# Chunks across four batches, states in place and one order table: a recurrence and a gated feed-forward layer in one kernel

## The chip, the cores and the metric

The kernel runs on one core of a Trainium2 chip. A core has TensorE (PE in the profile; PEld is its weight load), VectorE (DVE), ScalarE (ACT), GpSimd (POOL) and SyncE (SP), which here issues most of the DMAs. The engines run side by side, each through its own instructions in order, and wait for one another through semaphores. The metric is the device time of one execution in microseconds (us). The matrix products leave their results in PSUM, all else lies in SBUF.

## The reference

Inputs are `r`, `k`, `v`, `w` of shape (4 batches, 8 heads, 768 steps, 48) and `u`. A state of 48 x 48 per batch and head runs over the steps, and its output is the input of a gated feed-forward layer:

```python
state = np.zeros((B, H, D, D), dtype=np.float32)
for t in range(S):
    kt, vt, rt, wt = (k[:, :, t], v[:, :, t], r[:, :, t], w[:, :, t])
    cur = np.einsum('bhd,bhe->bhde', u[None] * kt, vt)
    y[:, :, t] = np.einsum('bhd,bhde->bhe', rt, state + cur)
    state = wt[:, :, :, None] * state + np.einsum('bhd,bhe->bhde', kt, vt)
x = y.transpose(0, 2, 1, 3).reshape(B * S, H * D)     # 3072 x 384
g = x @ w_gate                                        # 384 x 1536
return (g * (1.0 / (1.0 + np.exp(-g))) * (x @ w_val) @ w_out)
```

The weights of the layer come as 64-bit numbers.

## The kernel before

**Chunks.** The 768 steps of a batch are cut into 6 chunks of 128, so there are 24 chunks; chunk n here is chunk n % 6 of batch n // 6. The steps of a chunk, each a small function that takes n: loads `ws` (decays), `kr` (k and r, transposed), `nat` (k and r), `vt` (v); on VectorE `scan` (L287) and `scan2` (L304), running products of the decays from the end and from the start, between them `seed` (L296), which writes the reciprocal of the whole product into the first column of the tile `d1e`, from which `scan2` starts; `kq` and `re` scale k and r; ScalarE's `whole` keeps the whole product; `kb`, `kn` transpose k on TensorE and copy it out; `prod` (chunks 0 to 5) or `ru`, `ruk`, `a0` (the others) give the diagonal with `u`, `diag` (ScalarE) spreads it; `sc` (TensorE) makes the products of k and r, `pred` (VectorE) copies them over the diagonal under a mask; `sps` and `spb` decay the carried state and copy it for TensorE; `dl` and `st` add the chunk's part to it; `y` (TensorE) makes the chunk's output. `scan` reads the tile `d1q` and `scan2` the tile `d1e`; both are filled once.

**Products of the layer.** All products of the layer are made of two parts, a rounded value and its rest, in three matmuls. So `xh` (ScalarE) rounds `y` into the layer's input, and `xl` takes the rest, either on VectorE, or, for n < `TAKEN` = 10, by a matmul `xm` that subtracts the rounded part in PSUM and a copy on ScalarE. The 64-bit weights are turned into such pairs by the kernel, in 12 blocks f: `raw` (three DMAs), `top`, `low`, `upper` on ScalarE, `shift`, `sign`, `plus`, `lower` on VectorE. Two `raw` tiles take turns; one is free after `plus`.

**Groups.** The 24 chunks' outputs are put together in groups g of `GROUPS` = 4, 2, 4, 4, 4, 4, 2 tiles of 128 rows, as the moving side of the first products. For each group and each block f of 128 of the 1536 columns: `gv` (L534, 9 matmuls) twice, gate and value, 512 columns wide with four tiles and 256 with two; `silu` (ScalarE), `sg` (VectorE, times the value), `hh` and `hl` (the pair again), and `po` (L565), three matmuls of 384 columns for each tile, summed in PSUM over the 12 blocks. `ob` copies a finished tile out and `store` writes it. PSUM has two tiles for `gv`, four for `po` (lent to `sc` for the first four chunks), two for all of `kb`, `sc`, `dl` and `y`.

**Order.** `ORDER` (L47) names the steps in the order in which each engine and each DMA queue is to have them, for the start and groups 0 to 2. The steps that it names are kept in program order (`keep`, `pin`). `spin` are matmuls without use. From group 3 on, two Python loops (L624 to L654) issue the blocks, with the steps of the next group's chunks (`attention_steps`, `prepare`) between them; there only TensorE's order is pinned and the framework orders the rest. `check` takes the decays' bound for a flag; where the flag is set, a plain loop at the end computes all again. It overwrites `ws`, so for chunks 0 to 9 the loop loads `ws` a second time (`AGAIN`).

Of the kernel before, what the change touches and what calls it, by code (L numbers as in the profile page):

```python
# [52 lines left out]
scan:2 sign:1 whole:2 xh:1 vt:3 vz:2 kr:5 xm:1 spin:7 sps:2 xl:1 kq:2 spb:2 plus:1 kb:2 spin:5
seed:2 kn:2 raw:3 prod:3 upper:1 dl:2 spin:13 scan2:2 diag:2:1 st:2 ws:4 re:2 diag:2:0 lower:1
sc:2 spin:18 top:2 scan:3 low:2 pred:2:0 kq:3 vz:3 seed:3 whole:3 kb:3 pred:2:1 scan2:3 y:2 spin:4
kn:3 diag:3:0 shift:2 ws:5 re:3 vt:4 xh:2 sps:3 sc:3 diag:3:1 sign:2 xm:2 spin:8 spb:3 pred:3:0
xl:2 pred:3:1 top:3 dl:3 plus:2 y:3 spin:12 low:3 st:3 raw:4 scan:4 upper:2 vt:5 prod:4 xh:3
lower:2 vz:4 xm:3 spin:5 whole:4 xl:3 gv:0:0:0 kq:4 shift:3 seed:4 sign:3 gv:0:0:1 silu:0:0
scan2:4 top:4 plus:3 vz:5 ws:6 gv:0:1:0 low:4 re:4 raw:5 upper:3 sg:0:0 kb:4 scan:5 hh:0:0
gv:0:1:1 kn:4 lower:3 whole:5 diag:4:0 hl:0:0 diag:4:1 sc:4 seed:5 shift:4 po:0:0 sps:4 silu:0:1  # L60
sign:4 spb:4 top:5 sg:0:1 gv:0:2:0 plus:4 hh:0:1 low:5 hl:0:1 raw:6 pred:4:1 gv:0:2:1 upper:4
pred:4:0 silu:0:2 lower:4 po:0:1 sg:0:2 shift:5 hh:0:2 prod:5 dl:4 sign:5 gv:0:3:0 top:6 kq:5
low:6 st:4 gv:0:3:1 plus:5 hl:0:2 upper:5 raw:7 sps:5 kb:5 scan2:5 silu:0:3 po:0:2 nat:6 kn:5
diag:5:0 sg:0:3 ws:7 lower:5 hh:0:3 gv:0:4:0 hl:0:3 shift:6 re:5 po:0:3 silu:0:4 sign:6 top:7
scan:6 low:7 y:4 plus:6 whole:6 gv:0:4:1 diag:5:1 vt:6 seed:6 ru:6 raw:8 ruk:6 upper:6 a0:6 kr:6
gv:0:5:0 sg:0:4 nat:7 diag:6:0 lower:6 vz:6 hh:0:4 gv:0:5:1 shift:7 xh:4 spb:5 hl:0:4 sign:7
silu:0:5 po:0:4 top:8 sg:0:5 plus:7 hh:0:5 xm:4 gv:0:6:0 low:8 kq:6 raw:9 hl:0:5 upper:7 scan2:6
gv:0:6:1 silu:0:6 lower:7 ws:8 xl:4 re:6 sc:5 shift:8 po:0:5 sg:0:6 sign:8 hh:0:6 top:9 hl:0:6
gv:0:7:0 low:9 plus:8 scan:7 upper:8 raw:10 gv:0:7:1 pred:5:0 silu:0:7 whole:7 seed:7 lower:8
po:0:6 sg:0:7 shift:9 hh:0:7 gv:0:8:0 pred:5:1 sign:9 top:10 y:5 hl:0:7 low:10 plus:9 po:0:7  # L70
silu:0:8 kr:7 ru:7 upper:9 raw:11 ruk:7 a0:7 diag:6:1 lower:9 vt:7 kb:6 nat:8 gv:0:8:1 kn:6
shift:10 xh:5 diag:7:0 kq:7 xm:5 gv:0:9:0 sign:10 xl:5 sg:0:8 plus:10 hh:0:8 sc:6 top:11 gv:0:9:1
hl:0:8 pred:6:0 upper:10 pred:6:1 scan2:7 po:0:8 silu:0:9 low:11 lower:10 ws:9 vz:7 dl:6 ru:8 y:6
shift:11 gv:0:10:0 sg:0:9 diag:7:1 kr:8 vt:8 sign:11 hh:0:9 st:6 gv:0:10:1 plus:11 hl:0:9 upper:11
kb:7 re:7 po:0:9 silu:0:10 ruk:8 vz:8 lower:11 kn:7 a0:8 gv:0:11:0 sg:0:10 diag:8:0 nat:9 scan:8
hh:0:10 gv:0:11:1 sps:7 whole:8 kq:8 spb:7 seed:8 hl:0:10 scan2:8 silu:0:11 po:0:10 xh:6 ru:9
ws:10 re:8 ruk:9 xm:6 gv:1:0:0 sg:0:11 xl:6 a0:9 hh:0:11 gv:1:0:1 scan:9 nat:10 sc:7 hl:0:11
whole:9 seed:9 silu:1:0 po:0:11 pred:7:1 sg:1:0 pred:7:0 hh:1:0 ru:10 dl:7 ob:0:0 hl:1:0 gv:1:1:0
ob:0:1 ruk:10 out:0:0 out:0:1 st:7 y:7 sps:8 silu:1:1 po:1:0 diag:8:1 vt:9 kr:9 kb:8 gv:1:1:1
diag:9:0 a0:10 nat:11 gv:1:2:0 spb:8 sg:1:1 hh:1:1 gv:1:2:1 xh:7 hl:1:1 vz:9 silu:1:2 kn:8 po:1:1  # L80
sg:1:2 ob:0:2 kq:9 hh:1:2 out:0:2 xm:7 ob:0:3 gv:1:3:0 scan2:9 xl:7 out:0:3 sc:8 hl:1:2 ws:11 re:9
silu:1:3 po:1:2 ru:11 scan:10 gv:1:3:1 pred:8:1 whole:10 gv:1:4:0 seed:10 sg:1:3 ruk:11 hh:1:3
gv:1:4:1 pred:8:0 hl:1:3 dl:8 silu:1:4 po:1:3 st:8 sg:1:4 sps:9 hh:1:4 kb:9 y:8 hl:1:4 kn:9 po:1:4
diag:9:1 vt:10 kr:10 gv:1:5:0 diag:10:0 a0:11 gv:1:5:1 nat:12 silu:1:5 xh:8 gv:1:6:0 vz:10 sg:1:5
spb:9 xm:8 hh:1:5 gv:1:6:1 xl:8 hl:1:5 kq:10 silu:1:6 po:1:5 sg:1:6 scan2:10 hh:1:6 gv:1:7:0
hl:1:6 check:10 gv:1:7:1 ru:12 re:10 po:1:6 ruk:12 silu:1:7 ws:12 sg:1:7 scan:11 hh:1:7 gv:1:8:0
hl:1:7 gv:1:8:1 whole:11 seed:11 silu:1:8 gv:1:9:0 sg:1:8 hh:1:8 gv:1:9:1 hl:1:8 silu:1:9
gv:1:10:0 sg:1:9 gv:1:10:1 po:1:7 po:1:8 hh:1:9 hl:1:9 sc:9 silu:1:10 sg:1:10 hh:1:10 gv:1:11:0
pred:9:0 hl:1:10 gv:1:11:1 pred:9:1 silu:1:11 dl:9 sg:1:11 y:9 st:9 sps:10 po:1:9 spb:10 kr:11
vt:11 xh:9 po:1:10 hh:1:11 diag:11:0 hl:1:11 xm:9 po:1:11 xl:9 diag:10:1 kb:10 gv:2:0:0 kq:11  # L90
kn:10 a0:12 ob:1:0 scan2:11 nat:13 vz:11 ob:1:1 out:1:0 gv:2:0:1 silu:2:0 out:1:1 re:11 check:11
scan:12 gv:2:1:0 ws:13 sg:2:0 whole:12 seed:12 hh:2:0 ru:13 ruk:13 gv:2:1:1 hl:2:0 silu:2:1 po:2:0
sg:2:1 hh:2:1 hl:2:1 gv:2:2:0 po:2:1 silu:2:2 gv:2:2:1 gv:2:3:0 sg:2:2 hh:2:2 hl:2:2 gv:2:3:1
silu:2:3 po:2:2 sg:2:3 hh:2:3 hl:2:3 sc:10 po:2:3 pred:10:1 pred:10:0 dl:10 y:10 st:10 sps:11
gv:2:4:0 xh:10 kr:12 diag:12:0 vt:12 xl:10 spb:11 sc:11 silu:2:4 diag:11:1 gv:2:4:1 pred:11:0
kq:12 a0:13 vz:12 scan2:12 gv:2:5:0 nat:14 pred:11:1 check:12 re:12 kb:12 y:11 sg:2:4 kn:12 ws:14
scan:13 hh:2:4 gv:2:5:1 ru:14 whole:13 kr:13 diag:13:0 seed:13 vt:13 ruk:14 hl:2:4 xh:11 diag:12:1
xl:11 po:2:4 silu:2:5 a0:14 sg:2:5 nat:15 sc:12 kq:13 hh:2:5 vz:13 scan2:13 gv:2:6:0 hl:2:5
check:13 re:13 po:2:5 pred:12:0 silu:2:6 ws:15 pred:12:1 scan:14 dl:12 y:12 st:12 whole:14 seed:14
sps:13 kb:13 spb:13 kr:14 gv:2:6:1 vt:14 xh:12 kn:13 xl:12 diag:13:1 sc:13 sg:2:6 hh:2:6 gv:2:7:0  # L100
# [677 lines left out]
```

## Time and profile before

| | |
|---|---|
| three runs | 584.82, 585.49, 587.57 us; median 585.49 |
| the profiled execution: span | 585.2 us |
| mean granted TensorE clock | 0.993 |
| read from HBM, written | 45.04 MB, 4.72 MB |
| TensorE matmuls, spins among them | 5333, 160 |
| VectorE, ScalarE, GpSimd instructions | 511, 639, 11 |
| waits of VectorE's `sg` for `gv` | 138.3 us in 51 waits |
| waits of SP's `out` stores | 90.3 us for `ob` |

The page of the profile gives busy times over the whole span, a strip of 40 slices of 14.6 us each, and the groups of instructions. Matmuls are pipelined, so a matmul's own duration is longer than the time to the next one. The chain of waits, listed in order of time, merges runs of equal instructions: start, time, engine, line, count. A row of the timeline has start, duration, engine, line, operation, tiles and count. A row of a window has PE, PEld, DVE, ACT and POOL busy times with their counts, then the granted clock, DMA share and GB/s. A row of the waits has total us, number of waits and the longest.

### The profile page before, as it was taken

What the parts mean: (1) busy time and instruction counts of PE and PEld (TensorE: products, weight loads), DVE (VectorE), ACT (ScalarE), POOL (GpSimd) and SP (SyncE); (2) the same over time, 40 slices, a digit from 0 to 9 for tenths busy, and PEclk for the clock granted to TensorE, in tenths of its full rate; (3) what the DMA queues carried; (4) which work ended last, traced back from release to release, by engine and by line L of the source; (5) the groups of instructions that cost most, each with busy time, mean ns of one, the idle gap of its engine ahead of it and who ended that gap; (6) DMA issues with size and microseconds to landing.
All of it is one profiled execution on the core that took longest, in us unless ns stands there. A gap on an engine that the chain in (4) does not pass through costs nothing.

```text
span 585.2 us, 12525 instructions
## 1 busy us (share of the span) xinstructions
PE 570.4 (97%) x5333; PEld 494.4 (84%) x5333; DVE 325.1 (56%) x511; ACT 283.9 (49%) x639; POOL 1.8 (0%) x11
## 2 busy tenths in 40 slices
...
DVE  6999999995655349751456365446344332222221
...
GB/s 302 262 129 192 125 222 168 176 89 123 92 61 62 55 48 138 115 55 1 106 39 89 41 50 88 103 88 96 62 74 62 55 2 0 1 1 7 48 1 33
DMA packets 22334, 50.63 MB, mean 87 GB/s; under 512 B 2592, under 2 KB 8864, under 8 KB 22272
## 3 DMA queue, kind: packets, MB, share of 16 engines
...
q10 hardware_dynamic: 16, 0.00, 0.0%
HBM read 45.04 MB, written 4.72 MB: 85 GB/s over the span
## 4 chain that ended last, share of the span: by engine, by line
PE 83%; ACT 6%; DMA 5%; DVE 4%; issue 1%; SPq 0%; ACTq 0%; DVEq 0%
PE gv L541 46%; PE po L575 24%; PE y L441 5%; PE sc L385 4%; DMA raw<-in_wo_dram 2%; PE idle L608 2%; ACT at L346 1%; PE kb L361 1%; PE dl L409 1%; ACT raw L227 1%; DVE et L306 1%; DMA kr<-in_kr_dram 1%; DMA u_two<-in_u_rows_dram 1%; ACT raw L232 1%; ACT w_h L248 1%
## 5 line engine op out<-in xcount | busy, mean ns | idle before, releaser
L541 PE MATMUL gv<-xh,w_h 128*128 128x512 f32 (+1 forms) x504 | 183.7, 365 | 0.0
L541 PE MATMUL gv<-xl,w_h 128*128 128x512 f32 (+1 forms) x504 | 182.0, 361 | 0.0
L541 PE MATMUL gv<-xh,w_l 128*128 128x512 f32 (+1 forms) x504 | 181.6, 360 | 0.0
L553 DVE TENSOR_TENSOR sg<-sg,gv 128x512 f32<-128x512 f32 (+1 forms) x84 | 51.1, 608 | 141.4 <-PE gv L541 138.3
L541 PEld LDWEIGHTS gv<-xh,w_h 128*128 128x128 f32 x504 | 94.7, 188 | 15.1 <-issue 1.8
L541 PEld LDWEIGHTS gv<-xl,w_h 128*128 128x128 f32 x504 | 94.7, 188 | 15.0
L541 PEld LDWEIGHTS gv<-xh,w_l 128*128 128x128 f32 x504 | 94.8, 188 | 12.9
L575 PE MATMUL po<-w_h,hh 128*128 128x384 f32 x288 | 100.8, 350 | 0.5 <-ACT hh L558 0.5
L575 PE MATMUL po<-w_h,hl 128*128 128x384 f32 x288 | 97.2, 337 | 0.3 <-DVE hl L563 0.3
L558 ACT ACTIVATE hh<-sg 128x512 fp32r<-128x512 f32 (+1 forms) x84 | 47.8, 569 | 101.2 <-DVE sg L553 89.4
L575 PE MATMUL po<-w_l,hh 128*128 128x384 f32 x288 | 96.8, 336 | 0.0
L550 ACT ACTIVATE sg<-gv 128x512 f32<-128x512 f32 (+1 forms) x84 | 44.6, 531 | 90.8 <-PE gv L541 81.5
L563 DVE TENSOR_TENSOR hl<-sg,hh 128x512 fp32r<-128x512 f32 (+1 forms) x84 | 51.5, 613 | 51.1 <-ACT hh L558 50.7
L575 PEld LDWEIGHTS po<-w_h,hh 128*128 128x128 f32 x288 | 54.0, 188 | 7.5 <-issue 4.6
L575 PEld LDWEIGHTS po<-w_h,hl 128*128 128x128 f32 x288 | 54.1, 188 | 2.2 <-DVE hl L563 1.1
L575 PEld LDWEIGHTS po<-w_l,hh 128*128 128x128 f32 x288 | 54.0, 188 | 0.0
L346 ACT ACTIVATE at<-ident,a 128x128 f32<-128x128 f32 x144 | 45.6, 390 | 5.6 <-PE y L441 4.2
L390 DVE COPY_PREDICATED at<-mask,sc 128x512 f32<-128x512 uint32 x48 | 33.3, 730 | 8.7 <-PE sc L385 8.6
L317 ACT ACTIVATE ws<-ws 112x517 f32<-112x517 f32 x24 | 15.3, 638 | 35.3 <-DVE et L306 22.0
L289 DVE TENSOR_TENSOR_SCAN qt<-ws,d1q 112x516 f32<-112x516 f32 x24 | 29.4, 1226 | 1.8 <-DMA ws<-in_wt_dram 1.7
L306 DVE TENSOR_TENSOR_SCAN et<-ws,d1e 112x516 f32<-112x516 f32 x24 | 29.4, 1225 | 1.5 <-ACT pend L294 1.4
L385 PE MATMUL sc<-kr 48*64 48x128 f32 x768 | 28.6, 282 | 1.3 <-ACT kn L371 0.5
...
## 6 DMA issues: line engine op xcount, KB each, us to landing
...
raw<-in_gv_dram SPq DMA_DIRECT2D x24, 384.0 KB, 4.2
...
nat<-in_nat_dram SPq DMA_DIRECT2D x18, 384.0 KB, 3.1
raw<-in_wo_dram SPq DMA_DIRECT2D x12, 384.0 KB, 5.0
...
```

Source lines behind the costliest of these rows:

```text
L289: keep(nc.vector.tensor_tensor_scan(_flat(qts[n])[:, ::-1], wss[n][:, 1:][:, ::-1], _flat(d1q)[:, ::-1], 0.0, ALU.mult, ALU.add))
L306: keep(nc.vector.tensor_tensor_scan(_flat(ets[n]), wss[n][:, :L], _flat(d1e), 0.0, ALU.mult, ALU.add))
L346: keep(nc.scalar.activation(a[:, p, :], ident, AF.Copy, scale=d))
L385: pin(nc.tensor.matmul(scs[n][j][ms, p, :], krs[n][o, 0, p, ms], krs[n][o, 1, p, :], start=True, stop=True,))
L390: keep(nc.vector.copy_predicated(ats[n, j], mask4, scs[n][j]))
L441: pin(nc.tensor.matmul(ys[n][32 * q : 32 * q + 32, b // 4, :], lhs, rhs, start=start[q] == i, stop=stop[q] == i,))
L541: pin(nc.tensor.matmul(ps, a[:, f, j, q * P : (q + 1) * P], x[:, q, :], start=m == 0, stop=m == 3 * NK - 1,))
L550: keep(nc.scalar.activation(sgs[g, f], ps, AF.Silu))
L553: keep(nc.vector.tensor_tensor(sgs[g, f], sgs[g, f], gvs.pop((g, f, 1)), ALU.mult))
L558: keep(nc.scalar.activation(hhs[g, f], t, AF.Copy))
L563: keep(nc.vector.tensor_tensor(hls[g, f], t, hhs[g, f].bitcast(F32), ALU.subtract))
L575: pin(nc.tensor.matmul(pos[g][j], a[:, ts], x[:, f, 2, :], start=f == 0 and i == 0, stop=f == NF - 1 and i == 2,))
```

## The change

Chunk n now is chunk n // 4 of batch n % 4: the loads and the stores go through a list `place`, and the conditions on the chunk's place in its batch use n // 4. The four batches' states lie in four fixed tiles that `sps` and `st` change in place; `st` of the first four chunks is a copy on ScalarE. `ORDER` names all steps of the program to the last store, and the loops are gone. `TAKEN` is 6. In group 0 the first two blocks (f = 0, 1) are made in halves of 256 columns, `a` for tiles 0 and 1, `b` for tiles 2 and 3, and `po` can be named for one tile alone (`c0` to `c3`). One tile `d1` serves both scans: it holds ones in its last column, `seed` writes its first column, and a new step `zero` on GpSimd clears that column after `scan2`. The load of `u` stands at the start of the program; spins are 87. `check` loads `ws` again for 12 chunks (`ws2`, `check2`). The last group's second store goes through ScalarE's queue.

```diff
-TAKEN = 10
-AGAIN = 10
+TAKEN = 6
 ORDER = """
-spin:21 uh ws:0 kr:0 ws:1 kr:1 raw:0 vt:0 scan:0 vt:1 kr:2 ub:0 seed:0 whole:0 raw:1 prod:0 kq:0
...
+ws:0 kr:0 scan:0 prod:0 seed:0 kq:0 whole:0 scan2:0 ws:1 uh vt:1 kr:1 vt:0 re:0 zero:0 scan:1
+spin:23 kb:0 ws:2 raw:0 kr:2 kr:3 prod:1 kq:1 seed:1 kn:0 whole:1 diag:0:1 sc:0 diag:0:0 scan2:1
+zero:1 re:1 pred:0:1 pred:0:0 spin:7 kb:1 dl:0 scan:2 kn:1 vz:1 st:0 top:0 spin:5 dl:1 vz:0 low:0
+st:1 whole:2 sc:1 diag:1:0 spin:5 y:0 xh:0 prod:2 seed:2 shift:0 kq:2 sign:0 spin:16 xm:0 kb:2 raw:1
+top:1 diag:1:1 ws:3 plus:0 pred:1:0 scan2:2 pred:1:1 prod:3 re:2 kn:2 xl:0 vt:2 vz:2 upper:0 zero:2
+lower:0 scan:3 spin:15 y:1 kq:3 shift:1 diag:2:0 low:1 xh:1 dl:2 spin:16 xm:1 sc:2 diag:2:1 raw:2
+xl:1 low:2 vt:3 top:2 whole:3 kb:3 gv:0:0:0:a kn:3 silu:0:0:a seed:3 sign:1 pred:2:1 vz:3 plus:1
+scan2:3 pred:2:0 re:3 upper:1 diag:3:1 gv:0:0:1:a y:2 sg:0:0:a diag:3:0 hh:0:0:a xh:2 lower:1 sc:3
+pred:3:1 pred:3:0 shift:2 hl:0:0:a raw:3 st:2 vt:4 kr:4 ws:4 y:3 xh:3 sign:2 xm:2 xm:3 zero:3
+po:0:0:c0 xl:3 xl:2 po:0:0:c1 gv:0:0:0:b gv:0:0:1:b plus:2 upper:2 silu:0:0:b scan:4 top:3 seed:4
+lower:2 sg:0:0:b whole:4 hh:0:0:b ws:5 shift:3 hl:0:0:b sign:3 gv:0:1:1:a dl:3 gv:0:1:0:a silu:0:1:a
+low:3 sg:0:1:a po:0:0:c2 po:0:0:c3 hh:0:1:a prod:4 hl:0:1:a gv:0:1:1:b gv:0:1:0:b silu:0:1:b plus:3
+kq:4 po:0:1:a sg:0:1:b scan2:4 upper:3 hh:0:1:b vt:6 kr:5 raw:4 raw:5 top:4 hl:0:1:b lower:3
+gv:0:2:0 kb:4 low:4 silu:0:2 st:3 shift:4 kn:4 top:5 re:4 sign:4 plus:4 upper:4 po:0:1:b gv:0:2:1
...
+sg:6:10 hh:6:10 gv:6:11:0 gv:6:11:1 hl:6:10 silu:6:11 po:6:9 sg:6:11 hh:6:11 hl:6:11 po:6:10 out:5:3
+out:5:2 po:6:11:c0 ob:6:0 out:6:0 po:6:11:c1 ob:6:1 out:6:1
 """
...
-    d1q = cpool.tile([PR, NPR, C + 1], F32, tag="d1q", name="d1q")
-    nc.vector.memset(d1q, 0.0)
-    nc.vector.memset(d1q[:, :, C : C + 1], 1.0)
-    d1e = cpool.tile([PR, NPR, C + 1], F32, tag="d1e", name="d1e")
-    nc.vector.memset(d1e, 0.0)
+    d1 = cpool.tile([PR, NPR, C + 1], F32, tag="d1", name="d1")
+    nc.vector.memset(d1, 0.0)
+    nc.vector.memset(d1[:, :, C : C + 1], 1.0)
...
+    state = [cpool.tile([PR, NPR, D], F32, tag=f"st{b}", name=f"st_{b}") for b in range(B)]
...
+    place = [n % B * NCH + n // B for n in range(NC)]
...
+    def zero(n):
+        keep(nc.gpsimd.memset(d1[:, :, 0:1], 0.0))
...
     def sps(n):
-        carried[n] = state.pop(n - 1)
+        t = state[n % B]
         keep(nc.vector.tensor_tensor(
-            carried[n], carried[n], pend[:, n, :].unsqueeze(2).to_broadcast([PR, NPR, D]), ALU.mult,
+            t, t, pend[:, n, :].unsqueeze(2).to_broadcast([PR, NPR, D]), ALU.mult,
         ))
...
     def st(n):
-        state[n] = ap_.tile([PR, NPR, D], F32, tag="st", name=f"st_{n}")
-        if n % NCH == 0:
-            keep(nc.vector.tensor_copy(state[n], dls[n][:PR]))
+        t = state[n % B]
+        if n < B:
+            keep(nc.scalar.activation(t, dls[n][:PR], AF.Copy))
         else:
-            keep(nc.vector.tensor_tensor(state[n], dls[n][:PR], carried[n], ALU.add))
+            keep(nc.vector.tensor_tensor(t, dls[n][:PR], t, ALU.add))
...
+    def part(g, h):
+        tiles = GROUPS[g] if g in range(len(GROUPS)) else 1
+        return {"": (0, tiles), "a": (0, tiles // 2), "b": (tiles // 2, tiles)}[h]
+
+    def gv(g, f, j, h=""):
+        lo, hi = part(g, h)
+        ps = psM.tile([P, (hi - lo) * P], F32, tag="gv", name=f"gv_{g}_{f}_{j}{h}", bufs=2)
         m = 0
         for q in range(NK):
-            for a, x in ((w_h, x_h), (w_l, x_h), (w_h, x_l)):
+            for a, x in ((w_h, xs[g, 0]), (w_l, xs[g, 0]), (w_h, xs[g, 1])):
                 pin(nc.tensor.matmul(
-                    ps, a[:, f, j, q * P : (q + 1) * P], x[:, q, :], start=m == 0, stop=m == 3 * NK - 1,
+                    ps, a[:, f, j, q * P : (q + 1) * P], x[:, q, lo * P : hi * P],
+                    start=m == 0, stop=m == 3 * NK - 1,
                 ))
...
     def store(g, j, rows=None):
+        queue = nc.sync
         if rows is None:
-            t0 = (sum(GROUPS[:g]) + j) * P
+            t0 = place[sum(GROUPS[:g]) + j] * P
             rows = slice(t0, t0 + P)
-        keep(nc.sync.dma_start(out[rows, :], obs.pop((g, j))))
+            if g == len(GROUPS) - 1 and j % 2:
+                queue = nc.scalar
+        keep(queue.dma_start(out[rows, :], obs.pop((g, j))))
...
-    attention = attention_steps(sum(GROUPS[:FREE + 1]))
-    waiting = (FREE - 1, NF - 1)
-    again = list(range(AGAIN))
...
```

More of the change, by code (lines that the diff above doesn't have):

```diff
@@ L53 @@
[L53 to L100, printed above, removed]
```

317 lines of the change are left out of this document (165 added, 152 removed).

## The prediction

> **What bounds the kernel now.** I read the page's first two parts, then the busy time by windows, then the chain of waits in order of time for the pace of TensorE (PE), and last the instructions by line.
>
> ```profile
> span 585.2 us, 12525 instructions
> PE 570.4 (97%) x5333; PEld 494.4 (84%) x5333; DVE 325.1 (56%) x511; ACT 283.9 (49%) x639; POOL 1.8 (0%) x11
> ...
> DVE  6999999995655349751456365446344332222221
> ...
> 4.00:135.00 131.00, 127.60 (x1360) 106.84 (x1359) 124.50 (x162) 93.66 (x184) 0.00 (x0) 0.99 0.57 183
> 133.50:186.40 52.90, 52.88 (x677) 49.96 (x675) 28.41 (x58) 26.62 (x74) 0.00 (x0) 1.00 0.28 85
> ```
>
> PE is busy for 97% of the span, but in the first 135 us VectorE (DVE) is busy too, 124.5 of 131 us; from then on it has slack. Busy PE is not useful PE: the start is filled with `spin` matmuls, and overlapping matmuls count long. So I price PE's useful work by its pace in full stretches.
>
> ```profile
> 269.96 4.19 PE po L575 x24
> 489.94 4.12 PE gv L541 x18
> 541.26 2.11 PE gv L541 x18
> 354.32 1.67 PE y L441 x56
> ...
> 18.30 1.10 PE L385 MATMUL sc<-kr 48*64 48x128 f32 x32
> 14.86 0.54 PE L409 MATMUL dl<-vt,kn 128*32 128x48 f32 x32
> 52.87 0.26 PE L361 MATMUL kb<-ident,kr 112*128 112x112 f32 x1
> 53.98 0.48 PE L541 MATMUL gv<-xh,w_h 128*128 128x512 f32 x1
> ...
> L454 PE MATMUL y<-xh,minus 128*128 128x384 f32 x10 | 3.8, 377 | 1.5 <-ACT xh L450 1.5
> ```
>
> A `po` matmul costs 4.19/24 = 0.1745 us, a 512-column `gv` matmul 0.229, a 256-column one 0.117. A chunk costs `sc` 1.10, `y` 1.67 (32 of the 56 matmuls, about 0.96, where no state is carried in), `dl` 0.54, `kb` 1.1 with the sums (52.87 to 53.98) and half of that, 0.55, without (estimate), `xm` 0.38. Before: `gv` 5 x 216 x 0.229 + 2 x 216 x 0.117 = 297.8; `po` 864 x 0.1745 = 150.8; 24 `sc` 26.4; 20 x 1.67 + 4 x 0.96 = 37.2 for `y`; 20 `dl` 10.8; `kb` 14.3; 10 `xm` 3.8. The sum is 541.1 us, so 585.2 - 541.1 = 44.1 us of the span do no useful PE work. Where they lie:
>
> ```profile
> 3.89 1.23 DVE L289 TENSOR_TENSOR_SCAN qt<-ws,d1q 112x516 f32<-112x516 f32 x1 [1.71 <-DMA ws<-in_wt_dram]
> 46.59 0.48 PE L541 MATMUL gv<-xh,w_h 128*128 128x512 f32 x1
> 59.46 0.39 PE L541 MATMUL gv<-xh,w_h 128*128 128x512 f32 x1
> 133.47 0.28 PE L541 MATMUL gv<-xh,w_h 128*128 128x256 f32 x1
> 577.37 0.33 PE L575 MATMUL po<-w_l,hh 128*128 128x384 f32 x1
> ```
>
> The first `gv` starts at 46.6 with 18.4 us of useful work behind PE (4 `sc`, `y`, `kb`, `dl`, `xm`): 28.2 lost. Group 1 starts at 133.5 with 104.1 listed ahead of it: 29.4 lost, so only 1.2 more. From there to the last matmul's end at 577.7 are 444.2 us for 437.0 of work: 7.2 lost. The tail is 7.5. So 28 of the 44 us are the wait for the first `gv`.
>
> **The change, part by part.** *First blocks of 256 columns.* What the first `gv` waits for is DVE's queue:
>
> ```profile
> L245 DVE CUSTOM_DVE_ANT_0 s<-raw,s 128x2304 uint16<-128x2304 uint16 x12 | 16.6, 1383 | 0.0
> L241 DVE SCALAR_TENSOR_TENSOR s<-raw,s 128x1152 uint32<-128x1152 uint32 x12 | 16.2, 1350 | 0.0
> L251 DVE TENSOR_TENSOR w_l<-s,w_h 128x1152 fp32r<-128x1152 f32 x12 | 16.2, 1348 | 1.2 <-ACT w_h L248 1.2
> L289 DVE TENSOR_TENSOR_SCAN qt<-ws,d1q 112x516 f32<-112x516 f32 x10 | 12.2, 1223 | 1.7 <-DMA ws<-in_wt_dram 1.7
> L390 DVE COPY_PREDICATED at<-mask,sc 128x512 f32<-128x512 uint32 x14 | 9.8, 728 | 0.5 <-PE sc L385 0.4
> L237 DVE TENSOR_SCALAR s<-raw 128x1152 uint32<-128x1152 uint32 x12 | 9.1, 757 | 0.1
> ...
> L312 DVE TENSOR_TENSOR kr<-kr,et 112x512 f32<-112x512 f32 x9 | 6.2, 686 | 0.0
> ...
> L328 DVE TENSOR_TENSOR prod<-kr 112x512 f32<-112x512 f32 x6 | 4.1, 680 | 0.1
> ...
> L395 DVE TENSOR_TENSOR st<-st,pend 112x192 f32<-112x192 f32 x6 | 2.1, 347 | 0.0
> L297 DVE RECIPROCAL d1e<-qt 112x4 f32<-112x4 f32 x9 | 1.6, 173 | 0.0
> ```
>
> A chunk's preparation is 4.7 us (two scans of 1.22, `kq` taken as `re`, 0.69 each, `prod` 0.68, `seed` 0.17), two `pred` 1.46, a weight block 4.84 (0.757 + 1.350 + 1.383 + 1.348). Before, the table lists ahead of the first `gv` four chunks (18.8), eight `pred` (5.8), seven state steps (2.5), three weight blocks (14.5) and `scan:4`, `prod:4` (1.9): 43.4 us, and DVE took 46.6 - 3.9 = 42.7 for it. It was the bound. After, the list is three chunks (14.1), `scan`, `prod`, `kq` of the fourth (2.6), four `pred` (2.9), one weight block (4.8) and `shift:1` (0.8): 25.2. By that pace DVE is there at about 3.9 + 25.2 = 29; ScalarE (ACT) then still has `xh:1` and `xl:1` behind `diag`s, which I allow 1.5, so the first `gv` comes at about 30.5. PE has done 12.0 by then: 18.5 lost. Of the gain of 10 us part is given back at once. After two half products PE waits for `y:2` (behind `pred:2:0`) and `y:3` (behind `pred:3:0`), then for `po`, then for the `gv` buffers that `sg:0:1:b` frees, and DVE has 47.9 us listed ahead of that one: 3.9 + 47.9, so `gv:0:2:0` starts at about 52, with 27.9 us of useful work done. Lost: 24.1, against 59.46 - 31.0 = 28.5 at the same place before. From here to group 1 PE has 68.6 us of work, DVE 63.3 (before: 73.1 and 76.7, and PE took 74.0, 0.9 over). I take the same 0.9: group 1 starts at 52 + 68.6 + 0.9 = 121.5, **25.0 lost**. The 73 spins fewer bring nothing by themselves, as they fill time in which PE waits.
>
> Four half products cost 36 x (2 x 0.117 - 0.229) = 0.2 us more; four `xm` fewer (`TAKEN` 6) save 1.5. PE's total becomes **539.8**. The four `xl` go to DVE, about 0.5 each (estimate, 384 columns against the 512 of `re`), in group 1, where DVE has slack.
>
> *Chunks across batches, states in place.* PE's work per chunk is the same, and a state is needed four chunks later instead of one. Early on this removes the carried state from chunks 1 to 3. Later it removes waits that cost little, as ACT waited 2.9 us for states in all:
>
> ```profile
> ACT sp L403 <- DVE st L395: 2.9, 2, 2.0
> ```
>
> But DVE work moves: of chunks 6 to 8, which stood ahead of group 1, much now stands in it. DVE listed there goes from 32.3 us to 46.5, PE from 52.5 to 56.4. By the 28.4 busy us shown for 32.3 listed that is about 41 of 57, under the share of 95% in which PE lost 0.9 before. I leave the loss from group 1 on at **7.2**.
>
> *One seed tile.* `scan` of a chunk now waits for `zero` on GpSimd (POOL), which waits for `scan2` of the chunk before. No such memset is shown; its neighbours:
>
> ```profile
> 0.32 0.10 POOL L768 MEMSET const-float32-0.0<- 128x1 f32 x1 [0.32 <-issue]
> ...
> 1.45 0.26 POOL L192 MEMSET vz<- 128x192 f32 x1
> ...
> 2.19 0.29 POOL L176 TENSOR_SCALAR_AFFINE_SELECT mask<-mask 128x128 f32<-128x128 f32 x1
> 2.53 4.15 PEld L608 LDWEIGHTS <-mask 128*128 128x128 bf16 x21 [2.53 <-POOL mask L176]
> ```
>
> It takes 0.10 to 0.26; a hop from POOL is 0.05 (2.48 to 2.53), one to it I take the same. In every chunk `re` (0.69) at least stands on DVE between `scan2` and the next `scan`, twice alone, else 1.7 or more. The cover is at least 0.69 against at most 0.36: **nothing**. If `re` were late, the price is 0.4 a chunk. The Trainium skill ("SBUF — State Buffer", Who interferes with whom) says that VectorE and GpSimd share a port pair which a two-port VectorE instruction, such as `shift`'s kind can be, holds for its whole length. By it a `zero` that meets a `shift` starts up to 0.76 us later, and the sum would rise by that for a few early chunks at most; no run shows it yet, as POOL is idle after 2.5 us. The memset of `d1e` that goes (0.49) lies under the wait of 1.71 for `ws`: nothing.
>
> *SP's queue.* `raw:0` now stands behind `ws:2`, which waits for `ws:0`'s tile, that is for `scan2:0`. It goes out near 8.5 instead of 2.7, and lands about 5.0 later:
>
> ```profile
> L227 ACT ACTIVATE raw<-raw 128x1152 f32<-128x1152 f32 x12 | 16.1, 1340 | 5.1 <-DMA raw<-in_wo_dram 5.0
> ...
> raw<-in_wo_dram SPq DMA_DIRECT2D x12, 384.0 KB, 5.0
> ...
> SPq L220 <- DVE s L245: 36.0, 9, 7.6
> ```
>
> Issue and landing (8.5 + 1.4 for three issues + 5.0) and 1.34 for `top` make 16.3; DVE, with 12.9 us listed ahead, reaches `shift:0` at 16.8. Hidden by half a us; each us that it lands later is a us of DVE.
>
> *Order of the rest, second store.* Groups 3 to 6, ordered by loops so far, come under the table with the same work per group; what PE loses there is in the 7.2. The last store moves from SP to ACT's queue:
>
> ```profile
> 577.73 2.38 SPq L599 DMA_DIRECT2D out_dram<-ob  x2
> ...
> SPq L674 <- SPq L674: 2.6, 1, 2.6
> ```
>
> The second store holds SP until 580.1, and SP's 2.6 us behind it end late. With ACT issuing, SP is free some 1.8 earlier at best, and what ACT or the landing then holds up is not shown: between 0 and -1.8, I take the middle, -1.0, tail **6.5**.
>
> **Sum:** 539.8 + 25.0 + 7.2 + 6.5 = 578.5 against the span of 585.2. The median of the three runs, 585.49, stands 0.3 above the span, so 578.8. A measurement of this kernel can tell about 0.5%, 2.9 us.
>
> **Rivals.** *Better start* (17%): PE finds work between 30.5 and 52, if DVE runs ahead of its list. The loss is 18.5 + 0.9 = 19.4: 573.2. For it: 43.4 listed took 42.7. Against it: `pred`, `y`, `xm`, `xl` are a chain over three engines. *No gain at the start* (15%): the loss stays 29.4, as raw tiles come no faster: two buffers, each refilled only after `plus` (SP waited 36 us for it). Then 582.9, with the 0.3 583.2, no difference. *Slower* (10%): in group 1 the blocks are short (2.11 for both products), and DVE's queue, fuller by 14 us, puts one scan ahead of `sg` in each of 12 blocks; both `gv` buffers are full and PE waits 1.22 each time: 14.6, so 593.4. It decides from 0.56 us a block, where the gain of 6.7 is gone; against it, PE lost little in 133.5 to 186.4. *Half clock* (8%):
>
> ```profile
> 9.90:13.40 3.50, 3.33 (x40) 2.58 (x40) 3.07 (x6) 3.50 (x10) 0.00 (x0) 0.51 1.06 349
> ```
>
> Here PE ran at half clock for 3.5 us early on. With fewer spins this may come again between 31 and 42, where PE waits; one or two such stretches cost 1.7 each if full of work: 580.5 to 582.2. The Trainium skill ("TensorE: Matmul & The Clock Gate", What's actually happening) gives this as a gate that falls to half after an idle window of about 3.4 us; by it waits of 2 us, as I count them, leave the clock alone.
>
> **How the numbers follow.** The forecast holds 50%, its own range 575.5 to 582.5. The range 571 to 586 takes in every case but the slower one, and the unknown landing of `raw:0`. Faster: 50 + 17 + 7 of the half clock = 74%; same: 15 + 1 = 16%; slower 10%.
>
> **What would show it.** First `gv` near 30.5, third block near 52, group 1 near 121.5; no DVE wait for POOL; `top:0` before 16.5; PE idle in group 1 under 2 us; last matmul to end 6.5. A first `gv` after 40 or a group 1 after 127 makes it wrong at the start, DVE or ACT waits in group 1 over 7 us make it wrong behind.

## The result, and the profile after

| | median | lowest to highest | runs |
|---|---|---|---|
| the changed kernel | 577.20 us | 576.02 to 578.34 | 4 |
| the kernel before, beside it | 586.53 us | 584.82 to 588.73 | 4 |

The ratio is 0.9832, its 95% interval 0.98 to 0.9863: faster by 1.7%. The forecast was 578.8. Below are lines of the page of the changed kernel, from its first two parts.

```profile
span 576.5 us, 12483 instructions
...
PE 558.6 (97%) x5292; PEld 490.0 (85%) x5292; DVE 323.8 (56%) x514; ACT 277.4 (48%) x641; POOL 4.3 (1%) x34
...
DVE  6899899977676545454537554353555323422231
```

The share of busy PE is 97% as before, which again tells nothing of what was gained. DVE's strip does: before, it stood at 9 for eight slices and fell to 5 in the next one, where group 1 begins; now it comes down over 7 7 6 7 6 5. Part of DVE's work has moved from the start into group 1.

The milestones are read from the timeline of the changed kernel (start, duration, engine, line, operation, tiles, count; idle time before it in brackets):

```profile
5.58 5.09 PE L624 MATMUL idle<-mask 128*128 128x256 bf16 x23
8.50 0.31 SPq L325 DMA_DIRECT2D ws<-in_wt_dram  x1
8.86 0.90 SPq L274 DMA_DIRECT2D raw<-in_gv_dram  x2
10.46 0.39 PE L421 MATMUL kb<-ident,kr 112*128 112x112 f32 x1
16.87 1.28 ACT L281 ACTIVATE raw<-raw 128x1152 f32<-128x1152 f32 x1 [0.26 <-DMA raw<-in_wo_dram]
19.37 0.73 DVE L291 TENSOR_SCALAR s<-raw 128x1152 uint32<-128x1152 uint32 x1
21.79 0.65 PE L500 MATMUL y<-at,vz 128*32 128x128 f32 x5 [2.32 <-issue]
34.47 0.36 PE L549 MATMUL gv_0a<-x,w_h 128*128 128x256 f32 x1
54.09 0.40 PE L549 MATMUL gv<-x,w_h 128*128 128x512 f32 x1
124.08 0.28 PE L549 MATMUL gv<-x,w_h 128*128 128x256 f32 x1
570.50 0.34 PE L588 MATMUL po<-w_l,hh 128*128 128x384 f32 x1
```

With the unit prices of the prediction the span falls into its four terms again. Group 1 starts at 124.08 with 96.5 us of useful work listed ahead of it, so 27.6 are lost at the start. The last matmul ends at 570.84, 446.8 after that start, for 443.3 of work: 3.4 lost (rounded). The tail is 576.5 - 570.84 = 5.7.

| term, us | before | forecast | after |
|---|---|---|---|
| useful PE work | 541.1 | 539.8 | 539.8 |
| lost before group 1 | 29.4 | 25.0 | 27.6 |
| lost from group 1 on | 7.2 | 7.2 | 3.4 |
| tail | 7.5 | 6.5 | 5.7 |
| span | 585.2 | 578.5 | 576.5 |

The sum came out 2.0 from the span, but two terms were off by more than that, in opposite directions: the start 2.6 worse, the stretch behind it 3.8 better. The largest part of the gain of 8.7 us, 3.8, lies where the forecast had none. The profiled execution was the slowest of the four (578.34 us). A second profile of the same kernel (e12 below) has about 26.3 lost at the start, with the same 3.4 behind it and a tail of 5.6, so of the 2.6 at the start only 1.3 are there in both.

The waits of the changed kernel (total us, number, longest) and its windows (PE, PEld, DVE, ACT, POOL busy, granted clock, DMA share, GB/s) answer to the other steps:

```profile
POOL d L368 <- DVE et L363: 445.9, 23, 38.9
...
DVE kr L358 <- DMA kr<-in_kr_dram: 4.5, 3, 3.5
...
ACT sp L462 <- DVE st L454: 1.5, 3, 0.8
```

```profile
21.40:24.80 3.40, 3.01 (x17) 1.94 (x18) 3.26 (x4) 1.70 (x3) 0.00 (x0) 0.50 0.55 140
34.50:54.10 19.60, 16.45 (x222) 15.15 (x223) 18.94 (x25) 13.60 (x30) 0.11 (x1) 1.00 0.59 183
...
124.10:180.60 56.50, 56.50 (x804) 54.05 (x803) 40.47 (x78) 31.41 (x90) 0.42 (x4) 1.00 0.34 98
```

ACT waits for states for 1.5 us in the whole span. In group 1 PE never pauses, while DVE is busy for 40.47 of 56.50. Between the first `gv` and the third block DVE is busy for 18.94 of 19.60, so I take it as the bound there.

### The profile page after: what moved, and what is told of

It is laid out like the page before. It is cut to its first block, busy times and chain, and to the rows that moved or that the text cites. A ratio compares the mean times of both kernels' runs of the same rounds, so it can differ in the third digit from the quotient of the medians.

```text
span 576.5 us, 12483 instructions
## 1 busy us (share of the span) xinstructions
PE 558.6 (97%) x5292; PEld 490.0 (85%) x5292; DVE 323.8 (56%) x514; ACT 277.4 (48%) x641; POOL 4.3 (1%) x34
## 4 chain that ended last, share of the span: by engine, by line
PE 92%; DMA 3%; DVE 2%; issue 1%; ACT 1%; SPq 0%; DVEq 0%; ACTq 0%
PE gv L549 51%; PE po L588 26%; PE y L500 6%; PE sc L445 4%; PE idle L624 2%; DMA ws<-in_wt_dram 2%; PE kb L421 1%; DMA raw<-in_wo_dram 1%; PE dl L468 1%; DVE qt L346 1%; PE kb L423 0%; DVE at L450 0%; DVE w_l L305 0%; ACT raw L286 0%; DVE s L299 0%
## 5 line engine op out<-in xcount | busy, mean ns | idle before, releaser
L549 PE MATMUL gv<-x,w_h 128*128 128x512 f32 (+1 forms) x984 | 288.0, 363 | 1.0 <-ACT sg L559 1.0
L549 PEld LDWEIGHTS gv<-x,w_h 128*128 128x128 f32 x984 | 176.6, 188 | 32.2 <-issue 3.6
L549 PE MATMUL gv<-x,w_l 128*128 128x512 f32 (+1 forms) x492 | 176.7, 359 | 0.0
L549 PEld LDWEIGHTS gv<-x,w_l 128*128 128x128 f32 x492 | 92.5, 188 | 11.7
L588 PE MATMUL po<-w_h,hh 128*128 128x384 f32 x280 | 95.9, 343 | 0.0
L559 ACT ACTIVATE sg<-gv 128x512 f32<-128x512 f32 (+1 forms) x82 | 43.6, 531 | 87.7 <-PE gv L549 76.1
L450 DVE COPY_PREDICATED at<-mask,sc 128x512 f32<-128x512 uint32 x48 | 34.7, 739 | 17.3 <-PE sc L445 14.9
L346 DVE TENSOR_TENSOR_SCAN qt<-ws,d 112x516 f32<-112x516 f32 x24 | 29.4, 1226 | 5.1 <-DMA ws<-in_wt_dram 4.9
L363 DVE TENSOR_TENSOR_SCAN et<-ws,d 112x516 f32<-112x516 f32 x24 | 29.4, 1227 | 3.5 <-ACT pend L351 3.1
L500 PE MATMUL y<-at,vz 128*32 128x128 f32 x384 | 25.9, 275 | 2.3 <-issue 2.3
L445 PEld LDWEIGHTS sc<-kr 48*64 48x64 f32 x768 | 20.7, 132 | 5.9 <-issue 5.1
L500 PEld LDWEIGHTS y<-at,vz 128*32 128x32 f32 x384 | 21.1, 110 | 2.6 <-issue 2.6
```

Of the source, the lines that this page charges most:

```text
L346: keep(nc.vector.tensor_tensor_scan(_flat(qts[n])[:, ::-1], wss[n][:, 1:][:, ::-1], _flat(d1)[:, ::-1], 0.0, ALU.mult, ALU.add))
L363: keep(nc.vector.tensor_tensor_scan(_flat(ets[n]), wss[n][:, :L], _flat(d1), 0.0, ALU.mult, ALU.add))
L445: pin(nc.tensor.matmul(scs[n][j][ms, p, :], krs[n][o, 0, p, ms], krs[n][o, 1, p, :], start=True, stop=True,))
L450: keep(nc.vector.copy_predicated(ats[n, j], mask4, scs[n][j]))
L500: pin(nc.tensor.matmul(ys[n][32 * q : 32 * q + 32, b // 4, :], lhs, rhs, start=start[q] == i, stop=stop[q] == i,))
L549: pin(nc.tensor.matmul(ps, a[:, f, j, q * P : (q + 1) * P], x[:, q, lo * P : hi * P], start=m == 0, stop=m == 3 * NK - 1,))
```

## The experiments

The questions at the outset: is the first `gv` late through the spins that stand behind `uh` on PE, or, the rival, through the loads that stand behind `ws:2` on SP? And does the gain behind group 1 come from the table, with its fixed order, or from taking the chunks across the batches? Beside these, each part of the change is undone by itself, or done alone. The table has all of them, in us; the ratio is to the kernel before, run beside it. "Behind" is the time from the start of group 1 to the end of the last matmul.

| kernel | median | ratio, interval | first `gv` | third block | group 1 | behind | span |
|---|---|---|---|---|---|---|---|
| before | 585.49 | | 46.6 | 59.5 | 133.5 | 444.2 | 585.2 |
| changed | 577.20 | 0.9832 (0.98 to 0.9863) | 34.5 | 54.1 | 124.1 | 446.8 | 576.5 |
| e1 spins first | 577.16 | 0.9827 (0.9799 to 0.9854) | 35.0 | 54.3 | 123.0 | 446.8 | 575.4 |
| e2 no spins | 578.91 | 0.9848 (0.9826 to 0.987) | 36.0 | 56.5 | 125.3 | 446.8 | 578.0 |
| e3 whole blocks | 584.09 | 0.993 (0.9907 to 0.9954) | 47.8 | 62.9 | 132.8 | 446.8 | 585.1 |
| e5 batch by batch | 585.69 | 0.9972 (0.9956 to 0.9988) | 35.2 | 59.6 | 129.1 | 449.9 | 584.7 |
| e6 store on SP | 578.03 | 0.9856 (0.9823 to 0.9888) | 34.5 | 54.1 | 123.6 | 446.8 | 576.0 |
| e7 loads first | 572.94 | 0.9761 (0.9734 to 0.9788) | 30.5 | 50.4 | 119.6 | 446.8 | 571.8 |
| e8 whole, spins | 582.03 | 0.9923 (0.9896 to 0.995) | 43.5 | 57.9 | 127.7 | 446.8 | 580.2 |
| e9 across alone | 585.51 | 0.9985 (0.9968 to 1.0002) | 43.6 | 56.5 | 131.4 | 445.8 | 584.1 |
| e10 ten by `xm` | 578.32 | 0.9863 (0.9833 to 0.9893) | 34.6 | 54.7 | 124.1 | 447.8 | 577.7 |
| e11 late part free | 589.63 | 1.0055 (1.0036 to 1.0073) | 34.7 | 55.2 | 124.0 | 456.8 | 586.3 |
| e12 changed, again | 577.07 | 0.9845 (0.9814 to 0.9875) | 33.9 | 54.1 | 122.8 | 446.8 | 575.2 |

What two seed tiles would bring beside the four fixed states was not measured. The last row is the same kernel as the second, and the two profiles differ by 1.3 us, nearly all of it before group 1. A difference of that size at the start between two profiles means nothing by itself. A profile shows one execution, which need not be a middle one: that of e3 stands 2.8 us above its median, that of e11 1.5 below. The medians tell more: 577.20 and 577.07 for the same kernel.

### Spins ahead of the head transpose

```diff
-ws:0 kr:0 scan:0 ... zero:0 scan:1
-spin:23 kb:0 ws:2 ...
+spin:23 ws:0 kr:0 scan:0 ... zero:0
+scan:1 kb:0 ws:2 ...
```

> The first 23 spins stand ahead of uh on TensorE instead of behind it; nothing else is changed. In the changed kernel uh ran at 5.4 us, the 23 spins behind it at half clock from 5.6 to 10.5, and only then kb:0, though kq:0 had ended at 7.1. Theory 1 (spins on the path, and the cause of the late first gv at 34.5 instead of 30.5): kb:0 near 7.6, kn:0 near 9.3 instead of 12.1, then the landing of raw:0 (16.9) takes over, so the first gv comes at 32 to 33.5, and the span falls by 1 to 2.5 us to 574 to 575.5. Rival (the spins lie beside a wait on VectorE or on loads that ends last anyway): first gv stays within 34 to 35, span 576 to 577.

In the changed kernel 23 spins stand behind `uh` on PE and last from 5.58 on, so that `kb:0` comes at 10.46. Without that delay the timeline of e1 shows what is late next:

```profile
9.26 0.55 ACT L431 ACTIVATE kn<-kb 128x456 f32<-128x456 f32 x1 [1.33 <-PE kb L423]
16.84 1.25 ACT L281 ACTIVATE raw<-raw 128x1152 f32<-128x1152 f32 x1 [2.19 <-DMA raw<-in_wo_dram]
18.50 0.69 DVE L388 TENSOR_TENSOR prod<-kr 112x512 f32<-112x512 f32 x1 [2.29 <-DMA kr<-in_kr_dram]
24.73 1.22 ACT L281 ACTIVATE raw<-raw 128x1152 f32<-128x1152 f32 x1 [3.40 <-DMA raw<-in_wo_dram]
35.04 0.36 PE L549 MATMUL gv_0a<-x,w_h 128*128 128x256 f32 x1
```

`kn:0` starts at 9.26 instead of 12.08, but `top:0` starts at 16.84, as in the changed kernel, and ACT and DVE now wait 2.19, 2.29 and 3.40 us for `raw:0`, `kr:2` and `raw:1`. The first `gv` stays at 35, and the median of 577.16 is that of the changed kernel: theory 1 was wrong, the rival right. To take the spins out of the way gains nothing by itself, as three loads behind `ws:2` are late then.

### The loads ahead of `ws:2`

```diff
-... uh vt:1 kr:1 vt:0 re:0 ...
-... kb:0 ws:2 raw:0 kr:2 kr:3 ... kb:2 raw:1
+... uh vt:1 kr:1 vt:0 raw:0 kr:2 re:0 ...
+... kb:0 ws:2 raw:1 kr:3 ... kb:2
```

This is put on top of the spins' place in e1.

> The 23 spins stand ahead of uh, as in the run before, and on SP's queue raw:0 and kr:2 go ahead of ws:2, which waits for scan2:0, and raw:1 ahead of kr:3. With the spins alone moved, ScalarE waited 2.2 and 3.4 us for raw:0 and raw:1 and VectorE 2.3 for kr:2. Theory 2 (loads behind the waiting ws:2 are why the first gv is late): raw:0 is there by 12, raw:1 by 19, those waits go, the first gv comes at 30.5 to 32.5 and the span falls to 571.5 to 573.5. Rival (the chain over three engines for chunks 0 and 1 takes as long anyway): first gv at 34 or later, span 575 to 576.

The timeline of e7:

```profile
14.10 1.29 ACT L281 ACTIVATE raw<-raw 128x1152 f32<-128x1152 f32 x1
16.63 0.67 DVE L388 TENSOR_TENSOR prod<-kr 112x512 f32<-112x512 f32 x1
17.30 0.73 DVE L291 TENSOR_SCALAR s<-raw 128x1152 uint32<-128x1152 uint32 x1
20.38 1.31 ACT L281 ACTIVATE raw<-raw 128x1152 f32<-128x1152 f32 x1 [0.69 <-DMA raw<-in_wo_dram]
30.54 0.56 PE L549 MATMUL gv_0a<-x,w_h 128*128 128x256 f32 x1
50.40 0.40 PE L549 MATMUL gv<-x,w_h 128*128 128x512 f32 x1
```

The first two rows have no bracket: nobody waits for `raw:0` and `kr:2` any more, and ACT waits 0.69 for `raw:1` instead of 3.40. `shift:0` starts at 17.30 (16.8 in the forecast, 19.37 in the changed kernel), the first `gv` at 30.54, where the forecast had 30.5, and group 1 comes 4.5 us earlier than in the changed kernel, 3.5 earlier than in e1. The median of 572.94 is 4.3 below the changed kernel's, 4.2 below that of e1, and 2.4% below the kernel before. Theory 2 was right. The three loads were moved together, so what each is worth stays open.

### No spins

```diff
-spin:23 kb:0 ...
+kb:0 ...
```

and so for all seven entries, 87 matmuls.

> All 87 spins are left out; the useful work is unchanged. Theory 1 (spins buy clock): more of the windows before 40 us show half clock, sc and y of the first chunks take twice as long, the first gv comes at 35 or later, and the span grows by 2 to 4 us to about 579. Rival (spins only fill waits, and the first 23 stand in the way): first gv at 32 to 33.5, span 574 to 575.5, as with the spins moved.

The timeline of e2, at the start of `sc:0` and the first `gv`, and a window:

```profile
8.77 1.98 PE L444 MATMUL sc<-kr 48*64 48x128 f32 x32
35.97 0.56 PE L548 MATMUL gv_0a<-x,w_h 128*128 128x256 f32 x1
...
5.00:41.00 36.00, 27.31 (x345) 24.34 (x349) 28.41 (x37) 23.42 (x56) 0.42 (x4) 1.00 0.66 205
```

`sc` takes 1.98 us instead of 1.10, as at half clock. The window says 1.00 all the same: this trace holds no record of the clock before about 41 us, and the view shows that as full, so the clock is read from the durations here. In the three executions beside the profiled one the mean granted clock is 0.983 to 0.984, against 0.995 to 0.999 in the changed kernel. Group 1 starts 1.2 to 2.4 later than in the two profiles of the changed kernel, and the median is 1.7 higher (1.8 against e12). So the 87 spins are worth about 2 us, and durations and clock say that it is through the clock. Theory 1 was right, except that the windows don't show it.

### First blocks whole again

```diff
-kb:3 gv:0:0:0:a ... po:0:0:c0 ... po:0:0:c1 gv:0:0:0:b gv:0:0:1:b ...
+kb:3 ... gv:0:0:0 gv:0:0:1 ... po:0:0:c0 po:0:0:c1 po:0:0:c2 ...
```

The `:a` items go, and each `:b` item becomes the whole block. The second version has 34 spins besides, 22 ahead of `y:2` and 12 ahead of `y:3`.

> Group 0's first two blocks are made in one piece of 512 columns again, at the place where the b halves stand; the po of tiles 0 and 1 move behind the first hl. Theory 1 (the halves let TensorE do 2.1 us of gv and 1.0 of po while it waits for chunks 2 and 3, no more): first gv near 44.5, group 1 later by 1.5 to 3 us, span 578 to 579.5. Rival A (the halves are the whole gain of the start): group 1 later by 5 us or more, span over 581. Rival B (VectorE sets the pace there, halves bring nothing): within 0.7 of 576.5.

> The two whole blocks of 512 columns again, now with 22 spins ahead of y:2 and 12 ahead of y:3, where TensorE stood idle and the clock fell to a half from 36.9 to 50.6 us. Theory 3 (about 3 us of the loss of 8.6 without halves is the clock, the rest is work not done in the wait): no half clock after 36, group 1 at 129 to 131 instead of 132.8, span 581 to 583. Rival A (it is nearly all the clock): group 1 before 127.5, span under 579.5. Rival B (the clock cost nothing there): 584.5 or more.

Windows of e3 (columns as above), of the two stretches in which the clock was granted by half:

```profile
23.30:26.70 3.40, 3.40 (x19) 2.71 (x17) 1.92 (x3) 1.07 (x1) 0.10 (x1) 0.50 0.77 251
36.90:50.60 13.70, 9.56 (x104) 7.05 (x105) 10.75 (x13) 7.19 (x17) 0.10 (x1) 0.50 0.56 170
```

And the start of group 1 in the timeline of e8:

```profile
127.75 0.28 PE L547 MATMUL gv<-x,w_h 128*128 128x256 f32 x1
```

In the profile of e3, without the halves, group 1 starts at 132.8, 8.7 later than in the changed kernel: theory 1 (1.5 to 3 us) was wrong, rival A right. PE is busy for only 9.56 of the 13.70 us around the first `gv`, and the clock is at half for all of them. With spins in the pauses (e8) there is no half clock there, and group 1 starts at 127.7, earlier than theory 3 had it (129 to 131). So by the profiles 5.1 of the 8.7 us are clock, and 3.6 are work that the halves let PE do where it would wait.

But the profiled execution of e3 was its slowest of five, at 586.88 us with a mean granted clock of 0.984; the others have 583.05 to 584.16 at 0.989 to 0.993. By the medians the halves are worth 6.9 us (584.09 less 577.20). The spins of e8 give 2.1 of them back (582.03), and 4.8 are work. The clock's share lies between 2 and 5 us, then, and differs from one execution to the next.

### Chunks batch by batch

```diff
-    place = [n % B * NCH + n // B for n in range(NC)]
+    place = list(range(NC))
...
-        t = state[n % B]
-        if n < B:
+        t = state[n // NCH]
+        if n % NCH == 0:
```

In the table `sps` and `spb` of a chunk are listed behind `st` of the one before; all else keeps its place.

> The same table, but chunk n is again chunk n % 6 of batch n // 6; sps, spb, dl, st, kb and kn are listed where this needs them (sps of n+1 behind st of n, kb to st for 20 to 22 and none for the last chunks of a batch), everything else is at its place. Theory 1 (taking across batches saves little): about 1.5 us later at the first gv for the state of chunk 1 (0.35 + 0.72 + 0.7 on three engines), group 1 later by 1 to 2.5, the loss of TensorE from group 1 on up by at most 1 from its 3.4: span 578 to 580. Rival (it is what took the loss from group 1 on from 7.2 to 3.4): that loss goes back to 6.5 to 8, span over 580.5.

The timeline of e5 at the second half of the first block and at group 1, then its waits, first between 35 and 60 us, then from 124 us on:

```profile
50.48 0.28 PE L549 MATMUL gv_0b<-x,w_h 128*128 128x256 f32 x1
...
129.08 0.28 PE L549 MATMUL gv<-x,w_h 128*128 128x256 f32 x1
```

```profile
PE y L500 <- ACT sp L462: 3.5, 1, 3.5
...
ACT sp L462 <- DVE st L454: 22.2, 12, 6.1
```

The first `gv` keeps its place (35.2), but the second half starts 5.6 later, with a `y` waiting 3.5 for the carried state, and group 1 is 5.0 later (4.0 in lost time, as e5 has 1.0 more of work listed ahead). Behind group 1 ACT waits 22.2 us for states instead of 1.5 in all, and the stretch takes 449.9, with about 7.6 lost, about as much as in the kernel before. The span is 8.2 longer, and the gain over the kernel before shrinks to 0.3% (0.9972). Theory 1 was wrong, the rival right.

### Chunks across batches, in the order of before

```diff
-    d1q = ...
-    d1e = ...
+    d1 = ...
+    place = [n % B * NCH + n // B for n in range(NC)]
```

The kernel before with `place`, the states in place and one seed tile; of `ORDER` only the state steps are moved, and the loops from group 3 on remain.

> The kernel before with the chunks across the four batches, states in place and one seed tile (which makes the room for the four states), and nothing else of the change: its own order table, whole first blocks, loops, TAKEN 10. sps and spb of chunks 1 to 3 go, those of 6 and 12 and dl, st, kb, kn of 5 and 11 come. Theory 4 (across batches is worth 4 us ahead of group 1 and 4 behind it by itself, as the run without it said): first gv at 44 to 45.5 instead of 46.6, group 1 at 130 to 132, TensorE's loss behind it 3.5 to 5 instead of 7.2, span 578 to 581. Rival (it is worth that only to a table planned for it): span 583 to 586.

The timeline of e9 at the first `gv` and at group 1:

```profile
43.58 0.48 PE L541 MATMUL gv<-xh,w_h 128*128 128x512 f32 x1
...
131.43 0.28 PE L541 MATMUL gv<-xh,w_h 128*128 128x256 f32 x1
```

3.0 us are gained at the first `gv`, 2.0 are left at group 1, and the stretch behind is 1.6 longer. By the unit prices 103.2 us of useful work are listed ahead of its group 1, so about 7.9 are lost behind it: that loss did not fall at all, theory 4 was wrong and the rival right. Neither the table alone (e5) nor the batches alone lower it. The interval of the ratio, 0.9968 to 1.0002, takes in 1, that is no change. Across the batches alone, in an order not made for it, brings nothing that can be told; the new table without it brings 0.3%; both together 1.7%. Neither of the two single versions had an order planned for it, so what the best order of each would give stays open.

### Fixed order behind group 2

```diff
     for item in ORDER.split():
+        if item == "gv:3:0:0":
+            early[0] = False
```

From group 3 on only PE's order is then pinned, as in the loops of before.

> From gv:3:0:0 on, the steps are no longer kept in program order but for TensorE's own, as in the kernel before from group 3 on; the table is the same. Theory 5 (the smaller loss behind group 1 is the distance of four chunks between states, not the fixed order): from group 1 on 446 to 448 us as with the fixed order, span 576 to 578. Rival (the fixed order of the late groups is a part of the gain): 449 us or more, span over 578.5.

The waits of e11 between 270 and 580 us:

```profile
DVE kr L358 <- DMA kr<-in_kr_dram: 16.7, 8, 5.5
```

And a window of e11:

```profile
361.00:455.00 94.00, 89.91 (x775) 75.85 (x774) 42.64 (x70) 38.76 (x94) 0.42 (x4) 0.98 0.18 53
```

The stretch behind group 1 takes 456.8 instead of 446.8, and the kernel is slower than before (1.0055): theory 5 was wrong, the rival right. PE, which never pauses in that stretch of the changed kernel, is idle for 4.1 us in this window and for 5.7 in all, and the mean granted clock of the window is 0.98. By the medians e11 is 12.4 us slower than the changed kernel. DVE waits 16.7 us for `kr` loads, in the changed kernel 4.5; but the kernel before waits 17.6 for them in all and loses only 7.2 behind group 1, so that these waits are the cause is not shown. The fixed order is worth 10 us here, as this list of PE's steps goes with the order of the other engines. It doesn't show that any table gains 10 us over the loops of before, which lost only 7.2 in all.

### Second store on SP, ten chunks by `xm`, the same kernel again

```diff
-                queue = nc.scalar
+                queue = nc.sync
```

```diff
-TAKEN = 6
+TAKEN = 10
...
-... xl:6 ...
+... xm:6 xl:6 ...
```

and so for chunks 7 to 9.

> The last group's second store goes back to SP's queue; nothing else is changed. Theory 1 (the store's queue is what shortened the tail from 7.5 to 5.7): last matmul to end 6.7 to 7.5, span 577.5 to 578.3. Rival (the tail is set by other engines' ends): tail within 0.4 of 5.7.

> TAKEN is 10 again: chunks 6 to 9 get xm on TensorE, listed ahead of their xl, and xl as a copy on ScalarE instead of a subtraction on VectorE. Theory 1 (TensorE is the bound there, so its work counts in full): 4 x 0.38 = 1.5 us more behind the start of group 1, span 577.5 to 578.5. Rival (VectorE, freed of 2.2 us, gives it back): within 0.5 of 576.5.

> The changed kernel itself, once more, as a measure of what repeats. All theories: span 576 to 577.5, from group 1 on 446.8 us; the first gv within 1 us of 34.5, and a stretch of half clock of 3.4 us somewhere before 40 us.

The last store in the timeline of e6, and of the changed kernel, where ACT's queue issues it:

```profile
570.43 1.64 SPq L615 DMA_DIRECT2D out_dram<-ob  x2
```

```profile
571.47 0.39 ACTq L615 DMA_DIRECT2D out_dram<-ob  x1
```

With both stores on SP the tail (from the last matmul's end to the end of the span) is 5.6 us, no longer than the 5.7 with one: theory 1 was wrong, the rival right. Four more `xm` make the stretch behind group 1 longer by 1.0, 0.25 us each, where 1.5 was expected. The changed kernel, run again, has a median of 577.07 and the same 446.8 behind group 1, with a tail of 5.6; only its start differs, and its span of 575.2 lies under the 576 to 577.5 expected. Its records show no half clock between 10 us and the last matmul, where a stretch of 3.4 was expected.

## Why the prediction was right

*The first `gv`* (forecast 30.5, measured 34.5). The count of DVE's list was right, and e7 shows it: with the loads in time the first `gv` starts at 30.54. The step that failed is "Hidden by half a us; each us that it lands later is a us of DVE". `ws:2` went out at 8.50 as forecast, but `top:0`, which waits for `raw:0`, started at 16.87, 2.0 later than the 14.9 (8.5 + 1.4 + 5.0) that I had counted, and `shift:0` came 2.6 late. What DVE itself waited for ahead of `shift:0` is in two rows of its timeline in the changed kernel:

```profile
12.08 0.69 DVE L388 TENSOR_TENSOR prod<-kr 112x512 f32<-112x512 f32 x1 [1.56 <-PE kb L423]
18.68 0.69 DVE L388 TENSOR_TENSOR prod<-kr 112x512 f32<-112x512 f32 x1 [0.63 <-DMA kr<-in_kr_dram]
```

`prod:1` waited for `kb:0`, behind the spins, and `prod:2` for `kr:2`, which stands behind `raw:0` in the queue; `shift:0` follows without a wait. Where the spins are out of the way (e1), DVE comes earlier and waits 2.29 for `kr:2` alone, and ACT waits 3.40 for `raw:1`. I priced one load and not the queue behind it. By the medians of e1 and e7 the three loads cost 4.2 us.

*Part of the gain is given back at once*: right. Of the 12.1 us by which the first `gv` came earlier than before, 5.4 were left at the third block. Group 1 starts 9.4 earlier, but with 7.6 us less of work done (96.5 for 104.1), so in lost time the start gained 1.8. The 104.1 is 0.55 too high: it counts transposes for `kb:5`, which the kernel before leaves out for the last chunk of a batch (its trace has 27 of them ahead of group 1, 4 to a chunk, so 7 of the 8 chunks listed there have them). Without them the kernel before lost 30.0 at the start and 6.6 behind it, so the gains are 2.4 and 3.2 instead of 1.8 and 3.8.

*First halves.* The prediction didn't price them apart. They are worth 6.9 us by the medians (e3; 8.7 at group 1 of its slow profile), 2.1 of the 6.9 through the clock (e8; 5.1 of the 8.7 in the profiles). Without them the new table loses more at the start than the old one: 132.8 - 96.3 = 36.5 in the profile of e3, 31.4 in that of e8, against 29.4.

*Spins*: that the 73 fewer "bring nothing by themselves" is not tested by itself, but its reason, that spins only fill time in which PE waits, was wrong: the 87 that are left are worth about 2 us (e2), by the clock that they hold.

*Half clock*, a rival with 8%: it came at 21.4, for 3.4 us, not between 31 and 42, and in the second profile of the same kernel (e12) not at all. The mechanism is there, and it is what punishes e2 and e3. The Trainium skill ("TensorE: Matmul & The Clock Gate", What's actually happening) gives a free-running window of about 3.4 us: that agrees with stretches of 3.4 and 13.70 (four of 3.4), which begin at other times in other profiles (27.8 us in e1, 30.5 in e7, 36.9 in e3). It gives an idle window of that length as the condition: the trace differs, as the longest pause of PE in the 10 us ahead of 21.79 was the 2.32 in front of `y`.

*Across batches*: "removes waits that cost little" was the other step that failed. I counted only ACT's 2.9 us for states and left the loss behind group 1 at 7.2. It became 3.4, and without the change it is 7.6 (e5). In the new table the change is worth 4.2 us behind group 1 and 4.0 ahead of it; in the order of before it is worth nothing that can be told (e9). My reading is that the order of before gave the states room and that the new table, tighter ahead of group 1, has none; no run shows that apart.

*The slower rival*: DVE busy 40.47 us in group 1 (forecast about 41) and PE without a pause. Right.

*One seed tile*: `zero` takes 0.10 us, as this row of the changed kernel's timeline has it, and in the list of waits POOL waits for DVE, 23 times, and DVE not once for POOL among the rows shown. Right, at nothing.

```profile
8.53 0.10 POOL L368 MEMSET d<- 112x4 f32 x1 [6.04 <-DVE et L363]
```

The Trainium skill ("SBUF — State Buffer", Who interferes with whom) would let such a memset wait behind some of DVE's instructions; no row here shows a delay, and none was needed for the sum.

*Four `xm` fewer*: 1.5 forecast, 1.0 measured (e10).

*Tail*: 6.5 forecast, 5.7 measured, and the reason was wrong. The queue of the second store doesn't matter (e6). What shortened the tail by 1.8 against before stays open: in e9, which keeps the end of before, it is 6.9.

The time was forecast within 1.6 us by luck, then: a miss of 2.6 at the start was covered by 3.8 behind it and 0.8 in the tail. The 0.3 from span to median was luck too. It set the profile of one execution beside the median of several; where both are known of one execution, its time stands 1.7 to 2.6 us above its own span.
